# Reading k head by head in halves of TensorE's array, and loading the first down weights later, in linear attention with two feed-forward blocks

## The chip, the core and the metric

The kernel runs on one core of one Trainium2 chip. The metric is the device time of one execution in microseconds (us). A profile is one such execution, recorded instruction by instruction; its span runs from the first to the last instruction.

## What is computed

For 4 batches of 8 heads, 576 positions and 64 features a head, all in float32: linear attention with a norm per head, then a gated feed-forward block (d_ff 1536), then a softplus one (d_ff 2048).

```python
kv = np.einsum('bhsd,bhse->bhde', k, v)
out = np.einsum('bhsd,bhde->bhse', q, kv)
rms = np.sqrt(np.mean(out * out, axis=-1, keepdims=True) + 1e-06)
x = out / rms * g_norm                 # then (2304 tokens, 512 features)
x = (silu(x @ w_gate) * (x @ w_val)) @ w_out
y = softplus(x @ w2_in) @ w2_out
```

The weights arrive as 64-bit floats.

## The kernel before

**Attention.** The 576 positions of a batch are four chunks of 128 (position p*4+c is row p of chunk c) and a rest of 64. `load_kv` loads k and v in two halves of four heads. `kv_step(b, hp)` (lines 311 to 340) makes the head pair hp's part of `kv = k^T v`: four matmuls (line 318) with two heads of k as the stationary 128x128 operand and two heads of v as the moving one, and one (line 327) over the rest of 64 rows. That gives a 128x128 block of which only the two 64x64 blocks on the diagonal are wanted; after the last pair ScalarE copies one (line 338) and VectorE the other (line 339) into `kv`. Float32 matmuls appear as two matmul records each in the profile, so a step is 8 records of line 318 and 2 of line 327.

**The order of k.** A matmul's stationary operand needs the two heads of one chunk side by side. For batches 0 and 1 k is loaded as it lies in memory (tile `kr`, head, chunk, feature) and reordered into `k` by a ScalarE copy (line 185) and a VectorE copy three times as long (line 186), whose places in the order are set by the table `K0`. For batches 2 and 3 four loads of short runs (line 192) do the ordering.

**The chain of a chunk.** `q_step` transposes q (tile `pq`, copied by ScalarE to `qt`, line 353), `o_step` multiplies by kv (tile `pa`, line 366), ScalarE squares (line 377, `sq`), VectorE sums (lines 380 and 381, `ss`), GpSimd raises to a power (line 382, `rs`), VectorE scales (line 386, `x`), (for the rests of two batches together, `o_step` writes the one batch's 64 rows into output partitions 0 to 63 by eight matmul records, then the other's into 64 to 127 by eight more: shape 128*64, x16), and `x_step` transposes back (line 397, `px`) and splits into a high and a low part (`xh` line 403 on ScalarE, `xl` line 404 on VectorE). All products of the feed-forward blocks are three matmuls, high by high, low by high and high by low (`mm3`, line 436; `pg` gate, `pv` value, `py` down, `pz` the second block's down).

**Weights.** A weight tile (128x512, 512 KB) is loaded raw by `load_cols` or `load_rows` (tiles `gr`, `vr`, `or`), turned from 64-bit to float32 and split: ScalarE line 263, VectorE lines 266, 267 and 271 (`gz`, `vz`, `oz`), ScalarE line 282 (`gh`, `vh`, `oh`), GpSimd line 285 (`gl`, `vl`, `ol`). The raw tiles lie in the pool `stage`, of five buffers.

**What sets the order.** The program writes every engine's order out itself. Work off TensorE is put in a heap with a due time (`defer`), and TensorE's steps advance the clock of that heap by planned costs (`tick`). Batch 0's and half of batch 1's attention run first, by the tables; then `prepare` spreads the conversion of the down weights of chunk 0 and of the three tiles of chunk 1 over the time behind (`P0_AT`, `P0_EVERY`), and the feed-forward units of chunks 0 and 1 of a batch are woven with the attention of the next batches (`weave`). Loads are issued by SyncE (SP) in the order written; a load into a buffer waits for its last reader, and all loads behind it wait too.

Of the kernel before, what the change touches and what calls it, by code (L numbers as in the profile page):

```python
# [10 lines left out]
F32 = mybir.dt.float32  # L11
F32R = mybir.dt.float32r
I32 = mybir.dt.int32
I64 = mybir.dt.int64
# [4 lines left out]

K0 = [[4.0, 11.1], [16.08, 21.0]]
Q0 = [[9.4, 9.8, 10.2, 10.6], [25.0, 24.86, 25.4, 28.42]]
S0 = [6.5, 8.0, 12.9, 14.05, 10.7, 11.1, 11.5, 11.51, 14.9, 15.8, 15.78, 17.6, 23, 27.55, 25, 27.19]
S1 = [20.7, 21.9, 26.5, 27.76, 28]
# [12 lines left out]

P0_AT = 0.5
P0_EVERY = 2.09  # L40
P1_AT = 4.46
P1_EVERY = 9.21
SPLIT = 1.71
# [28 lines left out]
def tile_linear_attention_two_ffn(  # L72
# [19 lines left out]
    nc = tc.nc  # L92
    P = 128
    B, H, S, D = q.shape
# [34 lines left out]
    def defer(dt, f):  # L129
        heapq.heappush(queue, (now[0] + dt, next(serial), f))  # L130
# [29 lines left out]
    def load_kv(b, half):  # L160
        h0 = 4 * half
        if b == 1:

            if half == 0:
                kv_st["k", b] = accp.tile([P, 2, NC, 4, D], F32, tag="acc1", name="k1")
                kv_st["v", b] = xp.tile([P, 2, 4, NC * D], F32, tag="xh3", name="v1")
            kt, vt = kv_st["k", b][:, half], kv_st["v", b][:, half]
        else:
            pool, tag = (xp, f"x{'hl'[half]}2") if b == 0 else (stage, "stage")
            kt = pool.tile([P, NC, 4, D], F32, tag=tag, name=f"k{b}_{half}")  # L170
            vt = stage.tile([P, 4, NC * D], F32, tag="stage", name=f"v{b}_{half}")
        ks = k[b, h0:h0 + 4, 0:T, :]
        if b < 2:

            if b == 0:
                kr = xp.tile([P, 4, NC, D], F32, tag=f"x{'hl'[half]}4", name=f"kr{b}_{half}")
            else:
                if half == 0:
                    kv_st["raw"] = xp.tile([P, 2, 4, NC, D], F32, tag="xl3", name=f"kr{b}")
                kr = kv_st["raw"][:, half]  # L180
            nc.sync.dma_start(kr.rearrange("p h c d -> p h (c d)"), ks.rearrange("h (p c) d -> p h (c d)", p=P))
            ko = kr.rearrange("p h c d -> p c h d")

            def order():
                nc.scalar.copy(kt[:, 0:1], ko[:, 0:1])
                nc.vector.tensor_copy(kt[:, 1:NC], ko[:, 1:NC])

            defer(K0[b][half], order)
        else:
            ks = ks.rearrange("h (p c) d -> c p h d", p=P)  # L190
            for c in range(NC):
                nc.sync.dma_start(kt[:, c, :, :], ks[c])
        nc.sync.dma_start(vt, v[b, h0:h0 + 4, 0:T, :].rearrange("h (p c) d -> p h (c d)", p=P))
        kv_st["k", b, half] = kt
        kv_st["v", b, half] = vt

# [46 lines left out]
    def load_rows(w, nm, j):  # L243
        t = stage.tile([P, DM], I64, tag="stage", name=f"{nm}r{j}")
# [65 lines left out]

    def kv_step(b, hp):
        if hp == 0:
            kvps[b] = ps.tile([P, NP, P], F32, tag="ps", name=f"kvp{b}")
# [12 lines left out]
        j = 64 * (b % 2)  # L326
        nc.tensor.matmul(  # L327
            pk[:, hp, :],
            lhsT=r[0][j:j + 64, 2 * hp:2 * hp + 2, :].rearrange("p h d -> p (h d)"),
            rhs=r[1][j:j + 64, 2 * hp:2 * hp + 2, :].rearrange("p h d -> p (h d)"),  # L330
            start=False,
            stop=True,
        )
        tick(1.0)
        if hp == NP - 1:
            t = pages.tile([P, NP, P], F32, tag="pg", name=f"kv{b}")
            nc.gpsimd.memset(t, 0.0)
            nc.scalar.copy(t[0:64, :, 0:64], pk[0:64, :, 0:64])
            nc.vector.tensor_copy(t[64:128, :, 64:128], pk[64:128, :, 64:128])
            kvm[b] = t  # L340

    qts = {}
# [488 lines left out]
    with tc.manual_schedule():  # L831
# [65 lines left out]
        for t in range(NT - 1):  # L897
            if t + 1 < B:
                b = t + 2
                attn = side[t + 1][[len(S1), N2, N3][t]:]  # L900
                if b < B:
                    load_kv(b, 0)
                    load_kv_rem(b)
                    load_kv(b, 1)
                    load_q(b)
                    if b % 2:
                        load_q_rem(b // 2)
                    attn = attn + side[b][:[N2, N3][t]]
                weave(unit1(0, t) + unit1(1, t), (0, attn))
            else:  # L910
# [97 lines left out]
```

## Time and profile before

| | |
|---|---|
| median of 3 runs | 914.14 us (912.66 to 915.32) |
| profiled execution: device time | 911.74 us |
| profiled execution: span | 909.9 us |
| TensorE matmul (PE) busy | 885.3 us, 97% of the span |
| VectorE (DVE) busy | 589.3 us, 65% |
| ScalarE (ACT) busy | 353.0 us, 39% |
| GpSimd (POOL) busy | 288.2 us, 32% |
| chain that ended last, by engine | PE 85%, DVE 6% |

PE is the engine of the matmuls and PEld its loading of stationary operands. A row of the timeline gives start, duration, engine, line, operation, output tile and input tile; in brackets stands how long the engine was idle just before, and what ended that. The 24.6 us in which TensorE has no matmul lie for the larger part in the first 60 us.

### The profile page before, as it was taken

To read this page: it belongs to the slowest core of one execution; us is meant where nothing else is said; L and a number is where in the kernel's file an instruction comes from. 1 tells how busy PE (TensorE), PEld (TensorE's weight loads), DVE (VectorE), ACT (ScalarE), POOL (GpSimd) and SP (SyncE) were. 2 spreads that over 40 slices of the span, in tenths; PEclk is the share of its full clock that TensorE was granted. 3 is DMA by queue.
4 is the path that set the end of the run, shared out by engine and by line. 5 is a ranking of instruction groups with operands and counts; after the bars stand their busy time and mean duration, and the time that the engine had idled before them with its cause. 6 is when DMAs were issued, how large, how long until landed. Compare 5 with 4: busy or idle time off the path is not lost.

```text
span 909.9 us, 11710 instructions
## 1 busy us (share of the span) xinstructions
PE 885.3 (97%) x4352; PEld 741.3 (81%) x4352; DVE 589.3 (65%) x916; ACT 353.0 (39%) x615; POOL 288.2 (32%) x216
## 2 busy tenths in 40 slices
PE   6889999999999999999999999999998999999997
PEld 5668888888888888888888878888876888888886
DVE  2965357867778686778786745565688654545553
ACT  3634344332323323233333453444445443334340
POOL 0633211212122213131222453333544442444331
PEclk9999999999999999999999999999999999999999
DMA  9966202142342516060515043444433643333203
GB/s 271 254 138 125 93 1 70 47 162 88 121 151 81 169 63 208 1 231 24 185 69 210 24 138 139 139 155 165 167 126 129 232 138 139 106 127 107 103 1 115
DMA packets 83992, 114.00 MB, mean 125 GB/s; under 512 B 27616, under 2 KB 56288, under 8 KB 83680
## 3 DMA queue, kind: packets, MB, share of 16 engines
q1 hardware_dynamic: 83776, 113.27, 39.0%
q8 instruction: 34, 0.56, 0.3%
q14 instruction: 22, 0.18, 0.1%
q10 hardware_dynamic: 160, 0.00, 0.0%
HBM read 91.75 MB, written 21.50 MB: 124 GB/s over the span
## 4 chain that ended last, share of the span: by engine, by line
PE 85%; DVE 6%; issue 3%; POOL 2%; ACT 1%; DMA 1%; SPq 0%; POOLq 0%; DVEq 0%; ACTq 0%
PE pz L436 20%; PE pv L436 15%; PE pg L436 15%; PE py L436 15%; PE hY L436 8%; PE hZ L436 4%; PE hr L436 2%; PE hX L436 2%; PE pa L366 1%; PE kvp L318 1%; DMA kvr<-in_v_dram 1%; POOL b L620 1%; PE pq L349 1%; DVE yacc L496 1%; PE kvp L327 1%
## 5 line engine op out<-in xcount | busy, mean ns | idle before, releaser
L496 DVE TENSOR_TENSOR yacc<-yacc,py 128x512 f32<-128x512 f32 (+1 forms) x220 | 136.9, 630 | 53.7 <-PE py L436 53.1
L796 DVE TENSOR_TENSOR zacc<-zacc,pz 128x512 f32<-128x512 f32 x126 | 86.0, 684 | 109.4 <-PE pz L436 109.2
L698 POOL TENSOR_TENSOR gl<-c,gh 128x512 fp32r<-128x512 f32 x64 | 88.5, 1384 | 189.7 <-ACT gh L697 145.4
L436 PE MATMUL pz<-pl,gh 128*128 128x512 f32 x288 | 112.6, 391 | 2.0 <-POOL pl L285 2.0
L436 PE MATMUL pz<-ph,gl 128*128 128x512 f32 x288 | 112.5, 390 | 0.6 <-POOL gl L698 0.6
L436 PE MATMUL pz<-ph,gh 128*128 128x512 f32 x288 | 112.5, 391 | 0.0
L478 ACT CAST uh<-u 128x512 fp32r<-128x512 f32 (+1 forms) x60 | 34.7, 578 | 174.3 <-DVE u L475 174.3
L436 PE MATMUL hY<-b,wh 128*128 128x512 f32 x384 | 97.6, 390 | 0.9 <-DVE c L726 0.9
L436 PE MATMUL py<-uh,oh 128*128 128x512 f32 (+1 forms) x240 | 89.8, 374 | 1.3 <-DVE yacc L496 1.3
L436 PE MATMUL pv<-xh,vh 128*128 128x512 f32 (+1 forms) x240 | 90.1, 375 | 0.0
L436 PE MATMUL pg<-xh,gh 128*128 128x512 f32 (+1 forms) x240 | 90.0, 375 | 0.0
L436 PE MATMUL pg<-xl,gh 128*128 128x512 f32 (+1 forms) x240 | 88.6, 369 | 0.5 <-DVE xl L404 0.5
L436 PE MATMUL pv<-xh,vl 128*128 128x512 f32 (+1 forms) x240 | 88.7, 369 | 0.0
L436 PE MATMUL py<-uh,ol 128*128 128x512 f32 (+1 forms) x240 | 88.7, 369 | 0.0
L436 PE MATMUL pg<-xh,gl 128*128 128x512 f32 (+1 forms) x240 | 88.5, 369 | 0.0
L436 PE MATMUL py<-ul,oh 128*128 128x512 f32 (+1 forms) x240 | 88.4, 368 | 0.0
L436 PE MATMUL pv<-xl,vh 128*128 128x512 f32 (+1 forms) x240 | 88.4, 368 | 0.0
L436 PEld LDWEIGHTS hY<-b,wh 128*128 128x128 f32 x384 | 71.6, 188 | 15.8 <-DVE c L726 1.3
L436 PEld LDWEIGHTS pz<-pl,gh 128*128 128x128 f32 x288 | 54.2, 188 | 13.3 <-POOL pl L285 2.8
L436 PEld LDWEIGHTS pz<-ph,gl 128*128 128x128 f32 x288 | 54.1, 188 | 13.0 <-POOL gl L698 1.8
L479 DVE TENSOR_TENSOR ul<-u,uh 128x512 fp32r<-128x512 f32 (+1 forms) x60 | 38.9, 648 | 39.1 <-ACT uh L478 39.1
L436 PEld LDWEIGHTS pz<-ph,gh 128*128 128x128 f32 x288 | 54.2, 188 | 10.8 <-ACT ph L282 0.3
(115 smaller groups left out, 1644.3 us busy)
## 6 DMA issues: line engine op xcount, KB each, us to landing
pr<-in_moe_w_out_dram SPq DMA_DIRECT2D x32, 512.0 KB, 4.3
wh<-w2d SPq DMA_DIRECT2D x32, 512.0 KB, 4.2
wh<-w2d SPq DMA_DIRECT2D x64, 256.0 KB, 3.0
ir<-in_moe_w_in_dram SPq DMA_DIRECT2D x16, 512.0 KB, 5.9
w2d<-kh SPq DMA_DIRECT2D x32, 256.0 KB, 2.0
w2d<-kl SPq DMA_DIRECT2D x32, 256.0 KB, 2.5
gr<-in_moe_w_gate_dram SPq DMA_DIRECT2D x12, 512.0 KB, 5.7
vr<-in_moe_w_val_dram SPq DMA_DIRECT2D x12, 512.0 KB, 6.4
```

Source lines behind the costliest of these rows:

```text
L318: nc.tensor.matmul(pk[:, hp, :], lhsT=kt[:, c, i:i + 2, :].rearrange("p h d -> p (h d)"), rhs=vt[:, i:i + 2, c * D:(c + 1) * D], start=(c ...
L327: nc.tensor.matmul(pk[:, hp, :], lhsT=r[0][j:j + 64, 2 * hp:2 * hp + 2, :].rearrange("p h d -> p (h d)"), rhs=r[1][j:j + 64, 2 * hp:2 * hp ...
L349: nc.tensor.transpose(pq[:, hp, :], src[:, 2 * hp:2 * hp + 2, :].rearrange("p h d -> p (h d)"), ident)
L366: nc.tensor.matmul(pv[p0:p0 + n, hp, :], lhsT=qt[:, hp, p0:p0 + n], rhs=kvm[bb][:, hp, :], start=True, stop=True,)
L436: nc.tensor.matmul(dst, lhsT=a, rhs=b_, start=first and i == 0, stop=last and i == n - 1, skip_group_check=not check)
L478: nc.scalar.copy(uh, u)
L479: (nc.gpsimd if UL1 == "g" else nc.vector).tensor_sub(ul, u, f32(uh))
L496: defer(ADD1, lambda: nc.vector.tensor_add(a[:, d, :], a[:, d, :], p))
L620: (nc.gpsimd if BLO[n][int(i[1])] == "g" else nc.vector).tensor_sub(t[:, 1], src(), f32(t[:, 0]))
L698: nc.gpsimd.tensor_sub(lo, l, f32(hi))
L796: defer(ADD2, lambda: nc.vector.tensor_add(av[:, m, :], av[:, m, :], p))
```

## The change

Every batch's k is loaded as it lies in memory, in one load for a half, and the ordering copies of lines 185 and 186 and their table go. `kv_step` makes each head by itself: two matmuls of 64 stationary and 64 moving columns in the place of one of 128 and 128, the one head's into output partitions 0 to 63, the other's into 64 to 127. Of chunks 0 and 1 of the down weights the raw tiles are loaded behind the loads of the third batch, into the buffers of tile `xh2` and `xl2` and no longer into `stage`, and their conversion is due later (`O0_AT`, `O0_EVERY`); the gate and value weights of chunk 1 come earlier for it.

```diff
-K0 = [[4.0, 11.1], [16.08, 21.0]]
+O0_AT = 16.0
+O0_EVERY = 2.5
...
-            kt = pool.tile([P, NC, 4, D], F32, tag=tag, name=f"k{b}_{half}")
-            vt = stage.tile([P, 4, NC * D], F32, tag="stage", name=f"v{b}_{half}")
...
-            def order():
-                nc.scalar.copy(kt[:, 0:1], ko[:, 0:1])
-                nc.vector.tensor_copy(kt[:, 1:NC], ko[:, 1:NC])
...
-            for c in range(NC):
-                nc.sync.dma_start(kt[:, c, :, :], ks[c])
+            kt = pool.tile([P, 4, NC, D], F32, tag=tag, name=f"k{b}_{half}")
+            vt = stage.tile([P, 4, NC, D], F32, tag="stage", name=f"v{b}_{half}")
+        for t, src in ((kt, k), (vt, v)):
+            nc.sync.dma_start(
+                t.rearrange("p h c d -> p h (c d)"),
+                src[b, h0:h0 + 4, 0:T, :].rearrange("h (p c) d -> p h (c d)", p=P))
...
         for c in range(NC):
-            nc.tensor.matmul(
-                pk[:, hp, :],
-                lhsT=kt[:, c, i:i + 2, :].rearrange("p h d -> p (h d)"),
-                rhs=vt[:, i:i + 2, c * D:(c + 1) * D],
-                start=(c == 0),
-                stop=False,
-            )
+            for e in range(2):
+                nc.tensor.matmul(
+                    pk[D * e:D * e + D, hp, :],
+                    lhsT=kt[:, i + e, c, :],
+                    rhs=vt[:, i + e, c, :],
+                    start=(c == 0),
+                    stop=False,
+                )
...
-        load_rows(w_out, "o", 0)
         load_cols(w_gate, "g", 1)
         load_cols(w_val, "v", 1)
-        load_rows(w_out, "o", 1)
...
-        prepare(w1(0)[2:] + w1(1), None, P0_AT, P0_EVERY)
+        prepare(w1(1)[:2], None, P0_AT, P0_EVERY)
+        prepare([w1(0)[2], w1(1)[2]], None, O0_AT, O0_EVERY)
...
+                        load_rows(w_out, "o", 0, xp, "xh2")
+                        load_rows(w_out, "o", 1, xp, "xl2")
```

How that moves the instructions is seen at three places. On TensorE, at the first two head pairs of batch 2 among the value matmuls of chunk 1 (`pv`), before:

```order
L436 MATMUL pv_0_633<-xl_335,vh_476 128x512
L318 MATMUL kvp_640<-v_0_385,k_0_384 128x128 x4
L327 MATMUL kvp_640<-kvr_1_392,kvr_0_391 128x128
L436 MATMUL pv_0_633<-xh_334,vh_476 128x512
L436 MATMUL pv_0_633<-xh_334,vl_477 128x512
L436 MATMUL pv_0_633<-xl_335,vh_476 128x512
L318 MATMUL kvp_640<-v_0_385,k_0_384 128x128 x4
L327 MATMUL kvp_640<-kvr_1_392,kvr_0_391 128x128
```

and after:

```order
L421 MATMUL pv_0_642<-xl_350,vh_460 128x512
L302 MATMUL kvp_651<-v_0_410,k_0_409 64x64 x8
L312 MATMUL kvp_651<-kvr_1_414,kvr_0_413 64x64 x2
L421 MATMUL pv_0_642<-xh_349,vh_460 128x512
L421 MATMUL pv_0_642<-xh_349,vl_461 128x512
L421 MATMUL pv_0_642<-xl_350,vh_460 128x512
L302 MATMUL kvp_651<-v_0_410,k_0_409 64x64 x8
L312 MATMUL kvp_651<-kvr_1_414,kvr_0_413 64x64 x2
```

Nothing else moves on TensorE: each of the 16 steps has twice as many matmuls, of half the width, at the same place. On VectorE, at batch 1's chunks 1 to 3 (`x`, `ss`, `xl`), before:

```order
L266 TENSOR_SCALAR vz_478<-vz_478 128x512
L267 SCALAR_TENSOR_TENSOR vz_478<-vr_170,vz_478 128x512
L386 TENSOR_TENSOR x_1_509<-pa_1_443,rs_1_451 128x512
L271 SCALAR_TENSOR_TENSOR vz_478<-vr_170,vz_478 128x512
L404 SCALAR_TENSOR_TENSOR xl_522<-px_0_515,gcol,xh_521 128x4x128
L266 TENSOR_SCALAR oz_513<-oz_513 128x512
L267 SCALAR_TENSOR_TENSOR oz_513<-or_172,oz_513 128x512
L386 TENSOR_TENSOR x_2_540<-pa_2_469,rs_2_484 128x512
L380 TENSOR_REDUCE ss_3_534<-sq_3_533 128x8
L381 TENSOR_SCALAR ss_3_534<-ss_3_534 128x8
L271 SCALAR_TENSOR_TENSOR oz_513<-or_172,oz_513 128x512
L404 SCALAR_TENSOR_TENSOR xl_522<-px_1_554,gcol,xh_521 128x4x128
```

and after, from the same x of chunk 1 on:

```order
L371 TENSOR_TENSOR x_1_526<-pa_1_466,rs_1_474 128x512
L389 SCALAR_TENSOR_TENSOR xl_534<-px_0_528,gcol,xh_533 128x4x128
L371 TENSOR_TENSOR x_2_549<-pa_2_492,rs_2_503 128x512
L365 TENSOR_REDUCE ss_3_543<-sq_3_542 128x8
L366 TENSOR_SCALAR ss_3_543<-ss_3_543 128x8
L389 SCALAR_TENSOR_TENSOR xl_534<-px_1_561,gcol,xh_533 128x4x128
L371 TENSOR_TENSOR x_3_587<-pa_3_537,rs_3_544 128x512
L365 TENSOR_REDUCE ss_4_581<-sq_4_580 128x8
L366 TENSOR_SCALAR ss_4_581<-ss_4_581 128x8
L460 TENSOR_TENSOR u_0_592<-s_0_512,pv_0_521 128x512
L464 TENSOR_TENSOR ul_0_595<-u_0_592,uh_0_594 128x512
L389 SCALAR_TENSOR_TENSOR xl_534<-px_2_602,gcol,xh_533 128x4x128
```

No conversion stands between them any more; the six rows of `oz` now come together behind the last `xl` of batch 1, in front of chunk 1's `u` of batch 0. On SyncE's queue, from the loads of q's rest on, before:

```order
L230 DMA qr_163<-in_q_dram 64x8x64 x2
L245 DMA or_166<-in_moe_w_out_dram 128x512
L240 DMA gr_168<-in_moe_w_gate_dram 128x4x128
L240 DMA vr_170<-in_moe_w_val_dram 128x4x128
L245 DMA or_172<-in_moe_w_out_dram 128x512
L192 DMA k_0_384<-in_k_dram 128x4x64 x4
L193 DMA v_0_385<-in_v_dram 128x4x256
```

and after:

```order
L213 DMA qr_160<-in_q_dram 64x8x64 x2
L223 DMA gr_163<-in_moe_w_gate_dram 128x4x128
L223 DMA vr_165<-in_moe_w_val_dram 128x4x128
L174 DMA k_0_409<-in_k_dram 128x4x256
L174 DMA v_0_410<-in_v_dram 128x4x256
L187 DMA kvr_0_413<-in_k_dram 64x8x64
L187 DMA kvr_1_414<-in_v_dram 64x8x64
L174 DMA k_1_417<-in_k_dram 128x4x256
L174 DMA v_1_418<-in_v_dram 128x4x256
L205 DMA q_421<-in_q_dram 128x8x64 x4
L228 DMA or_426<-in_moe_w_out_dram 128x512
L228 DMA or_428<-in_moe_w_out_dram 128x512
```

The two down weights have moved behind all of batch 2, and a half of k is one load in place of four.

## Rows read from the trace of the kernel before

**Rows 1.** The page: busy us, share and count; busy tenths in 40 slices.

```profile
PE 885.3 (97%) x4352; PEld 741.3 (81%) x4352; DVE 589.3 (65%) x916; ACT 353.0 (39%) x615; POOL 288.2 (32%) x216
...
PE   6889999999999999999999999999998999999997
```

**Rows 2.** Two stages of 10 us: length, busy us of each engine, granted clock, DMA.

```profile
40.00:50.00 10.00, 8.83 (x64) 7.12 (x63) 8.67 (x16) 7.41 (x14) 6.87 (x5) 1.00 0.85 172
50.00:60.00 10.00, 6.70 (x38) 5.21 (x37) 7.57 (x13) 4.07 (x7) 6.56 (x5) 1.00 0.97 172
```

**Rows 3.** Timeline of TensorE, 34 to 59 us: three of its waits.

```profile
35.04 0.50 PE L436 MATMUL pg<-xl,gh 128*128 128x512 f32 x1 [0.50 <-DVE xl L404]
...
47.60 0.66 PE L397 MATMUL px<-ident,x 128*128 128x128 f32 x4 [0.44 <-DVE xl L404]
...
58.33 0.66 PE L397 MATMUL px<-ident,x 128*128 128x128 f32 x4 [3.30 <-DVE x L386]
```

**Rows 4.** Chain that ended last: matmuls of batch 0's kv (start, us, what).

```profile
9.89 2.00 PE kvp L318 x8
...
16.18 0.90 PE kvp L318 x8
...
18.58 0.43 PE kvp L327 x2
```

**Rows 5.** Timelines of VectorE and GpSimd, 11 to 31 us.

```profile
11.91 0.76 DVE L218 COPY q<-qr 128x512 f32<-128x512 f32 x2 [6.23 <-DMA qr<-in_q_dram]
...
28.81 0.94 DVE L186 COPY k<-kr 128x768 f32<-128x768 f32 x1
29.67 1.28 DVE L386 TENSOR_TENSOR x<-pa,rs 128x512 f32<-128x512 f32 x2
...
27.85 1.94 POOL L382 TENSOR_TENSOR rs<-ss,mhalf 128x8 f32<-128x8 f32 x1 [0.18 <-DVE ss L381]
```

**Rows 6.** Timelines of PE, ACT, DVE and POOL, 48 to 58 us: batch 1's rest.

```profile
48.88 1.58 PE L366 MATMUL pa<-kv,qt 128*64 128x128 f32 x16
...
51.05 0.62 ACT L282 CAST oh<-oz 128x512 fp32r<-128x512 f32 x1 [1.96 <-DVE oz L271]
...
53.16 0.68 DVE L380 TENSOR_REDUCE ss<-sq 128x8 f32<-128x512 f32 x1
...
55.19 1.64 POOL L382 TENSOR_TENSOR rs<-ss,mhalf 128x8 f32<-128x8 f32 x1 [0.17 <-DVE ss L381]
...
57.59 0.68 DVE L386 TENSOR_TENSOR x<-pa,rs 128x512 f32<-128x512 f32 x1
```

**Rows 7.** Tile oz, 34 to 56 us: durations in ns, least, median, most.

```profile
L266 DVE TENSOR_SCALAR oz<-oz x2: 422/630/837, 35.8 to 47.5; 128x512 int32<-128x512 int32 x2
L267 DVE SCALAR_TENSOR_TENSOR oz<-or,oz x2: 691/692/693, 36.3 to 48.3; 128x512 int32<-128x512 int32 x2
L271 DVE SCALAR_TENSOR_TENSOR oz<-or,oz x2: 684/686/687, 38.2 to 50.3; 128x512 int32<-128x512 int32 x2
```

**Rows 8.** Chain that ended last, where TensorE never waits.

```profile
90.59 0.70 PE pv L436 x3
91.29 0.89 PE kvp L318 x8
92.18 0.41 PE kvp L327 x2
92.60 0.89 PE py L436 x3
...
115.09 1.51 PE pa L366 x16
```

**Rows 9.** Tile pa in two short stretches: matmul and load records present.

```profile
115.07:115.51 0.44, 0.44 (x5) 0.44 (x5) 0.00 (x0) 0.00 (x0) 1.00 0.00 0
115.51:115.90 0.39, 0.39 (x10) 0.39 (x9) 0.00 (x0) 0.00 (x0) 1.00 0.00 0
```

**Rows 10.** Timeline of SyncE's queue: q of batch 2.

```profile
47.36 4.97 SPq L222 DMA_DIRECT2D q<-in_q_dram  x4
```

More of the change, by code (lines that the diff above doesn't have):

```diff
@@ L164, in load_kv @@
             if half == 0:
-                kv_st["k", b] = accp.tile([P, 2, NC, 4, D], F32, tag="acc1", name="k1")
-                kv_st["v", b] = xp.tile([P, 2, 4, NC * D], F32, tag="xh3", name="v1")
+                kv_st["k", b] = accp.tile([P, 2, 4, NC, D], F32, tag="acc1", name="k1")
+                kv_st["v", b] = xp.tile([P, 2, 4, NC, D], F32, tag="xh3", name="v1")
             kt, vt = kv_st["k", b][:, half], kv_st["v", b][:, half]
         else:
-            pool, tag = (xp, f"x{'hl'[half]}2") if b == 0 else (stage, "stage")
-            kt = pool.tile([P, NC, 4, D], F32, tag=tag, name=f"k{b}_{half}")
-            vt = stage.tile([P, 4, NC * D], F32, tag="stage", name=f"v{b}_{half}")
[L172 to L182, printed above, removed]
-            def order():
-                nc.scalar.copy(kt[:, 0:1], ko[:, 0:1])
-                nc.vector.tensor_copy(kt[:, 1:NC], ko[:, 1:NC])
-            defer(K0[b][half], order)
-        else:
-            ks = ks.rearrange("h (p c) d -> c p h d", p=P)
-            for c in range(NC):
-                nc.sync.dma_start(kt[:, c, :, :], ks[c])
-        nc.sync.dma_start(vt, v[b, h0:h0 + 4, 0:T, :].rearrange("h (p c) d -> p h (c d)", p=P))
+            pool, tag = (xp, f"x{'hl'[half]}4") if b == 0 else (stage, "stage")
+            kt = pool.tile([P, 4, NC, D], F32, tag=tag, name=f"k{b}_{half}")
[4 more added lines that the diff above has]
+                src[b, h0:h0 + 4, 0:T, :].rearrange("h (p c) d -> p h (c d)", p=P))
         kv_st["k", b, half] = kt
@@ L241, in load_cols, with load_rows @@
         raw[nm, j] = t.rearrange("p c f -> p (c f)").bitcast(I32).rearrange("p (n t) -> p n t", t=2)
-    def load_rows(w, nm, j):
-        t = stage.tile([P, DM], I64, tag="stage", name=f"{nm}r{j}")
+    def load_rows(w, nm, j, pool=None, tag="stage"):
+        t = (pool or stage).tile([P, DM], I64, tag=tag, name=f"{nm}r{j}")
         nc.sync.dma_start(t, w[j * P:(j + 1) * P, :])
@@ L312, in kv_step @@
         if hp == 0:
-            kvps[b] = ps.tile([P, NP, P], F32, tag="ps", name=f"kvp{b}")
+            kvps[b] = ps.tile([P, NP, D], F32, tag="ps", name=f"kvp{b}")
         pk = kvps[b]
@@ L317, in kv_step @@
         for c in range(NC):
-            nc.tensor.matmul(
-                pk[:, hp, :],
-                lhsT=kt[:, c, i:i + 2, :].rearrange("p h d -> p (h d)"),
-                rhs=vt[:, i:i + 2, c * D:(c + 1) * D],
-                start=(c == 0),
-                stop=False,
-            )
+            for e in range(2):
[6 more added lines that the diff above has]
+                )
         r = kvr[b // 2]
         j = 64 * (b % 2)
[L327 to L333, printed above, removed]
+        for e in range(2):
+            nc.tensor.matmul(
+                pk[D * e:D * e + D, hp, :],
+                lhsT=r[0][j:j + 64, 2 * hp + e, :],
+                rhs=r[1][j:j + 64, 2 * hp + e, :],
+                start=False,
+                stop=True,
+            )
         tick(1.0)
@@ L337, in kv_step @@
             nc.gpsimd.memset(t, 0.0)
-            nc.scalar.copy(t[0:64, :, 0:64], pk[0:64, :, 0:64])
-            nc.vector.tensor_copy(t[64:128, :, 64:128], pk[64:128, :, 64:128])
+            nc.scalar.copy(t[0:64, :, 0:64], pk[0:64])
+            nc.vector.tensor_copy(t[64:128, :, 64:128], pk[64:128])
             kvm[b] = t
@@ L907, in tile_linear_attention_two_ffn @@
                         load_q_rem(b // 2)
+                    else:
+                        load_rows(w_out, "o", 0, xp, "xh2")
+                        load_rows(w_out, "o", 1, xp, "xl2")
                     attn = attn + side[b][:[N2, N3][t]]
```

## Prediction

> **What bounds the kernel now.** I read first the page: TensorE's matmuls are busy 97% of the span, and its row of slices is full from the fourth slice (68 us) almost to the end [rows 1]. Behind that point only less TensorE time can shorten the kernel; ahead of it TensorE waits, and what it waits for counts. The windows of 10 us show how much: between 50 and 60 us it has matmuls for 6.70 us, 3.30 idle, and between 40 and 50 for 8.83 [rows 2]. The timeline of TensorE then names the waits: 0.50 us until the last `xl` of batch 0, 0.44 us until an `xl` of batch 1, and 3.30 us until an `x` [rows 3]. The last is the x of batch 1's rest, whose transpose stands behind chunk 1's gate matmuls; all of the idle time of that window is this one wait. The shorter waits between these are for ScalarE's copies of q; a gate or value conversion takes the down one's place ahead of those copies, so I leave them as they are.
>
> **The sum, part by part.**
>
> *A. Ordering copies.* The VectorE copies of batch 0 stand where VectorE has nothing else to do, and the transposes of q that follow are held by q itself: q's copies end at 11.91 + 0.76 = 12.67 us [rows 5]. The second half of batch 1's copies does count. It takes 28.81 to 29.67 on VectorE, and only then come the two x, the second at 30.27 us (half of the 1.28 us later) [rows 5]. It can't come as early as the copy is long, since it needs the fourth `rs`: that ends at 29.79 and itself waited 0.18 us for VectorE's `ss` [rows 5], which the other half's copy delays. So the x can come at 29.79 - 0.18 = 29.6 and not at 30.27: 0.6 us, which all of batch 0's `xl` and the 0.50 us wait [rows 3] pass on. Bounds: 0.5 (no gain on `ss`) to 0.9 (the whole copy).
>
> *B. The second half of batch 0's kv.* From 16.18 to 18.58 + 0.43 = 19.01 us TensorE works on two steps, 2.83 us [rows 4], and the copies of kv, the first products and GpSimd's chain of `rs` hang behind them. What a step costs afterwards is the disputed price of this change, so first that.
>
> *The price of a step in halves.* Before, 8 records take 0.89 us, 0.111 each; the two of the rest 0.41 where 2 x 0.111 = 0.22 would do; and the next three products 0.89 where they take 0.70 elsewhere [rows 8]. So a change of the array's shape costs 0.19 us, and there are two of them in a step: 0.89 + 0.41 + 0.19 = about 1.50 us. Afterwards there are three, as the four chunks (128 rows by 64 columns) and the rest (64 by 64) differ from the big products and from each other: 0.57 us, and 16 + 4 = 20 records of some length t each, so 0.57 + 20t. A record of 64 moving columns should take half of one of 128: 0.055 us. Whether the two halves of the array work at one time decides the rest. The one place where this trace uses halves is the product of the rests: 16 records, eight in the one half and then eight in the other, in 1.51 us [rows 8], where 16 x 0.111 + 0.19 = 1.97 would be one after the other. The short windows show where that comes from: in 0.44 us while only the first half works there are 5 matmuls and 5 loads, in the 0.39 us where the two meet 10 and 9 [rows 9]. Matmuls and loads of the two halves go on beside each other, at twice the rate. The new order alternates between the halves after every two records, better than eight and eight. So t has bounds of 0.028 (fully beside each other) and 0.055 (one after the other); I take 0.030, near the lower, because that is what the meeting half of those rows does. A step is then 0.57 + 0.60 = 1.17 us, 0.33 less than 1.50.
>
> The Trainium skill, in "TensorE: Matmul & The Clock Gate", section "Part 3: Packing small matmuls", says that loads overlap with matmuls in flight only when the row group differs, and here the two halves share all rows. By that rule a load and a matmul of 0.055 each would follow one another, t = 0.11, and a step would cost 2.8 us. The trace disagrees where it can be asked: in the second window loads and matmuls of two column halves fill the same 0.39 us [rows 9].
>
> *B, then.* Two steps next to each other have four changes of shape within and 40 records: 0.76 + 40t = 1.96 us at t = 0.030, 0.9 less than 2.83. At t = 0.055 it is 2.96, a loss of 0.1. The first two steps of batch 0 are hidden by q's arrival (above), batch 1's four by the chain of A; were that cover gone, each would be worth the same 0.33.
>
> *C. Conversions of the down weights.* Two tiles cost VectorE 2 x (0.63 + 0.69 + 0.69) = 4.0 us between 35 and 51 us [rows 7], in a stretch where it is busy 8.67 of 10 us [rows 2], and they stand in the chain to the long wait: the product of the rests ends at 48.88 + 1.58 = 50.46; ScalarE's cast of `oh` waits 1.96 us for `oz` and only starts at 51.05, and the square stands behind it; `ss` starts at 53.16, `rs` at 55.19 behind GpSimd's two low parts, the x at 57.59 [rows 6]. Without the conversions I rebuild the chain, with 0.62 us for each step on ScalarE, 0.68 for each on VectorE and 1.64 for `rs`, as the cast, the `ss`, the x and the `rs` of [rows 6] take: square, `ss`, then on VectorE chunk 0's u, its low part (a cast on ScalarE between) and an `xl`, beside which `rs` is done, then x. That is 2 x 0.62 + 5 x 0.68 = 4.6 us and, estimated, 0.5 for the small step behind `ss` and the hand-overs: 5.2 us from the product's end to the transpose, against 58.33 - 50.46 = 7.9 before; TensorE has 58.33 - 3.30 - 50.46 = 4.6 us of its own to do in that time. So 0.6 of the 3.30 us stays and 2.7 is gained; bounds 1.5 (`rs` still queued behind one low part of 1.3) and 3.3. The 0.44 us before it waits for an `xl` that stands directly behind a value conversion; with that done earlier I count it as gained: 0.4.
>
> The 4.0 us of conversions now stand behind the last `xl` of batch 1, in front of chunk 1's u. That u needs the value product, whose 12 matmuls (0.23 us each [rows 8]) lie behind the transpose with batch 2's four steps (1.2 each) among them: 7.5 us, so 3.5 us of cover. If that went, u and the down product behind it would be late by as much. Their loads are queued behind batch 2's q, four issues in 4.97 us [rows 10]. The v ahead of q now waits for the buffer of the gate weight, whose last step takes the place of the first `oz` one, 38.2 + 0.7 = 38.9 us [rows 7]; with 5 us for q the two are issued near 45 us. They are wanted near 54, where TensorE ends chunk 1's gate product; what a load takes to land isn't in these rows, but it has 9 us.
>
> *D. The eight steps of batches 2 and 3.* They lie where TensorE never waits: 8 x 0.33 = 2.6 us. At t = 0.055: 0.57 + 1.10 = 1.67, a loss of 8 x 0.17 = 1.4. The single loads of k cost nothing on this path, as those steps already found k there.
>
> Sum: 0.6 + 0.9 + 2.7 + 0.4 + 2.6 = 7.2 us. The profiled execution, 911.74 us with a span of 909.9, would take 904.5; it lies 2.4 below the median of the runs, 914.14, from which the sum gives **906.9 us**. I call 0.3%, 2.7 us, the least that a measurement tells from no change: below 911.4 is faster, above 916.9 slower.
>
> **The rivals.**
>
> *Halves one after the other* (t = 0.055). Everything of A and C comes (3.7), B loses 0.1 and D 1.4: 2.2 us gained, 911.9 us, no change by the bound. For it speaks that no row here shows records as short as 64 columns; against it rows 9.
>
> *A sequencer that can't hand out records so fast.* A step is 40 instructions with the loads; the closest that records stand in this trace is about 0.055 us in the meeting stretch [rows 9]. If handing out is the limit, t lies at 0.055 or somewhat above, and the time near the last rival's. The Trainium skill, same page, section "Back-to-back issue gap", gives 62 ns a matmul with hardware decode off; by that the gain would be 0.8 us and the time 913.3. No row here decides it.
>
> *Slower.* A record in halves can't hide its load and keeps today's 0.109 to 0.111 us. Then eight steps cost 0.57 + 20 x 0.109 = 2.75 each, 10.0 us more, and B 0.76 + 4.36 - 2.83 = 2.3 more; with A and C's 3.7 back that is 8.6 slower, 922.7 us. The general form is a loss of 200t - 9.5 against 3.7 gained: from t = 0.066 on the change is no gain, from 0.080 slower by the bound.
>
> *The long wait hardly shrinks*, because `rs` on GpSimd and not VectorE holds it: C 1.5 in place of 2.7, 908.1 us.
>
> *A cold start.* The granted clock is 1.00 in the rows that I read [rows 2, 9], yet eight records take 2.00 us at 9.89 and 0.90 at 16.18 [rows 4]: until then TensorE works at the lower of its two levels, 1.2 of 2.4 GHz. Shorter matmuls between 6 and 12 us leave more idle time before q arrives, and the rise could come later. If batch 0's products (32 records, 3.6 us at the full level) fell to the lower level by half, the chain to `rs` starts 1 to 2 us later: 908 to 909 us.
>
> **How the numbers follow.** Likeliest, as summed: 0.58, its own range 904.5 (t = 0.028, the long wait gone, a run at the quick end of those shown) to 908.5. Long wait hardly shrinks: 0.10; cold start: 0.06. Halves in series or handing out as the limit: 0.20, of which a fifth falls just below 911.4. Slower: 0.06. Faster is then 0.58 + 0.10 + 0.06 + 0.04 = 0.78, the same 0.16, slower 0.06. The range reaches from 904.0 to 912.0, up to the rival of halves in series.
>
> **What would show it.** Right: a step among the big products as one row of 16 records in well under 0.7 us and one of 4; the transpose of batch 1's rest waiting under 1 us; batch 0's first `pg` with `xl` near 33.5 us and not 35.04; TensorE's busy time lower by about 2 to 3 us behind 60 us. Wrong: 16 records in 0.9 us or more (series), gaps of "issue" within them (handing out), or that transpose still idle for 2 us with GpSimd named.

## The result, and the profile after

The changed kernel takes 905.33 us (median of 4 runs, 904.67 to 906.78) beside 913.4 us for the kernel before in the same session: ratio 0.9912, 95% interval 0.9889 to 0.9935, so faster by 8.1 us. Run again on another chip (the ninth kernel below) it took 906.53 us, ratio 0.9938 (0.9923 to 0.9953). The gain differs between the two sessions (8.1 and 4.9 us) mostly through the kernel before, whose runs differ with TensorE's mean granted clock: in the second session it took 911.06 to 911.46 us in six runs at a mean of 1.000 and 914.72 in one at 0.995, in the first none is below 912.14. The profiled execution after took 905.19 us with a span of 903.4, 6.5 less than before.

The page of the kernel after, TensorE's busy time and its slices, answers to [rows 1]; the windows under it to [rows 2] (length, busy us of PE, PEld, DVE, ACT and POOL, granted clock, DMA share, GB/s).

```profile
PE 877.4 (97%) x4512; PEld 732.4 (81%) x4512; DVE 585.0 (65%) x912; ACT 351.6 (39%) x611; POOL 288.0 (32%) x216
...
PE   5799999999999999999999999999998999999997
```

```profile
20.00:30.00 10.00, 7.65 (x102) 6.56 (x100) 9.04 (x18) 4.55 (x8) 8.23 (x6) 1.00 1.12 319
30.00:40.00 10.00, 7.18 (x53) 5.67 (x52) 6.87 (x13) 5.83 (x11) 2.44 (x3) 0.83 0.99 257
40.00:50.00 10.00, 9.27 (x68) 7.66 (x67) 7.21 (x13) 6.23 (x11) 8.40 (x6) 1.00 1.05 260
50.00:60.00 10.00, 9.65 (x86) 7.20 (x86) 8.02 (x14) 5.40 (x9) 1.88 (x3) 1.00 0.19 62
```

Between 50 and 60 us TensorE has work for 9.65 us where it had 6.70, and between 40 and 50 for 9.27 where it had 8.83: term C. But between 30 and 40 the granted clock is 0.83, a mean over its two levels, and TensorE has 2.8 us without a matmul where it had 1.2. The timeline of TensorE shows both (brackets: idle time just before, and what ended it); it answers to [rows 3].

```profile
18.96 3.84 PE L351 MATMUL pa<-kv,qt 128*128 128x128 f32 x32 [0.99 <-DVE kv L324]
...
31.54 0.66 PE L334 MATMUL pq<-ident,q 128*128 128x128 f32 x4 [0.54 <-ACT q L201]
33.80 0.80 PE L421 MATMUL pg<-xh,gh 128*128 128x512 f32 x1 [1.60 <-ACT xh L388]
...
34.82 0.64 PE L421 MATMUL pg<-xl,gh 128*128 128x512 f32 x1
35.26 1.87 PE L351 MATMUL pa<-kv,qt 128*128 128x128 f32 x8
...
47.39 0.60 PE L382 MATMUL px<-ident,x 128*128 128x128 f32 x4
...
48.62 1.58 PE L351 MATMUL pa<-kv,qt 128*64 128x128 f32 x16
...
55.11 0.66 PE L382 MATMUL px<-ident,x 128*128 128x128 f32 x4 [0.35 <-DVE x L371]
```

The wait of 3.30 us is 0.35, and the one of 0.44 is gone. The transpose of batch 1's rest starts at 55.11 and not 58.33: 3.22 us. But the first gate product `pg` starts at 33.80, where it started at 33.83 before, and with `xl` at 34.82 for 35.04, not near 33.5: of the 1.5 us of A and B 0.2 has arrived there. In front of it stands a new wait of 1.60 us, and the eight records of `pa` take 1.87 us where they take 1.13 elsewhere.

Behind 60 us the chain of work shows a step among the big products, which answers to [rows 8]:

```profile
86.49 0.61 PE kvp L302 x16
87.10 0.26 PE kvp L312 x4
87.36 0.89 PE py L421 x3
88.25 0.61 PE kvp L302 x16
```

That is 0.61 + 0.26 + 0.19 (the three products behind take 0.89 for 0.70) = 1.06 us for 1.50, so 0.44 less in each, 8 x 0.44 = 3.5 us: term D. With 3.22 that makes 6.7 of the 6.5 us by which the span is shorter.

Where A and B went is read from three timelines (ScalarE, VectorE, GpSimd), which answer to [rows 5] in the first three lines and to [rows 6] in the last three:

```profile
30.87 0.62 ACT L201 COPY q<-qr 128x512 f32<-128x512 f32 x1 [2.72 <-DMA qr<-in_q_dram]
...
28.43 0.69 DVE L371 TENSOR_TENSOR x<-pa,rs 128x512 f32<-128x512 f32 x1 [0.33 <-POOL rs L367]
...
30.87 0.74 DVE L201 COPY q<-qr 128x512 f32<-128x512 f32 x1 [1.08 <-DMA qr<-in_q_dram]
...
50.30 0.60 ACT L362 ACTIVATE sq<-pa 128x512 f32<-128x512 f32 x1 [1.48 <-PE pa L351]
...
50.93 0.69 DVE L365 TENSOR_REDUCE ss<-sq 128x8 f32<-128x512 f32 x1
...
54.37 0.68 DVE L371 TENSOR_TENSOR x<-pa,rs 128x512 f32<-128x512 f32 x1
```

The last x of batch 0 comes at 28.43 us, earlier than the 29.6 that A alone promised, so A and B were there at this point. B can be seen at its source too: batch 0's first products start at 18.96 us, and before at 19.97. Then ScalarE and VectorE stand still, ScalarE for 2.72 us, for batch 1's q, whose copies are ahead of the next `xh` and `xl` in their order. The loads are later than before. From issue to landing the tile qr takes (least, median, most) before, and then after:

```profile
DMA to landing us min/median/max: 8.0/10.1/10.7
```

```profile
DMA to landing us min/median/max: 8.6/12.4/12.5
```

The view of the DMA queues shows one more piece there: code of an engine, 16 KB in one packet. Before it falls in the window 28 to 30 us, after in 20 to 22 (queue: packets, MB, share of 16 engines):

```profile
q8 instruction: 1, 0.02, 4.3%
```

```profile
q8 instruction: 1, 0.02, 3.6%
```

3.6% of 16 engines over 2 us is 1.15 us on one of them, in a stretch where the DMA engines are busy throughout (share 1.12 between 20 and 30 us). What is queued behind it on that engine would end as much later; q comes 1.8 us later (12.5 for 10.7), so the piece by itself doesn't account for all of it. This was not in the prediction; runs 8, 10 and 11 below bear on it.

### The profile page after: what moved, and what is told of

Its sections match the earlier page's. It is cut to its first block, busy times and chain, and to the rows that moved or that the text cites. A ratio compares the mean times of both kernels' runs of the same rounds, so it can differ in the third digit from the quotient of the medians.

```text
span 903.4 us, 12017 instructions
## 1 busy us (share of the span) xinstructions
PE 877.4 (97%) x4512; PEld 732.4 (81%) x4512; DVE 585.0 (65%) x912; ACT 351.6 (39%) x611; POOL 288.0 (32%) x216
## 4 chain that ended last, share of the span: by engine, by line
PE 85%; DVE 4%; issue 3%; ACT 2%; POOL 2%; SPq 2%; DMA 1%; POOLq 0%; DVEq 0%; ACTq 0%
PE pz L421 20%; PE pv L421 15%; PE pg L421 15%; PE py L421 15%; PE hY L421 8%; PE hZ L421 4%; PE hr L421 2%; PE hX L421 2%; PE pa L351 2%; DMA qr<-in_q_dram 1%; SPq L174 1%; POOL b L605 1%; PE px L382 1%; POOL gl L683 1%; DVE yacc L481 1%
```

## The experiments

Times are medians, each beside the kernel before on the same chip. Batch and term names are the prediction's.

**1. Only the down weights late** (C alone: copies of k and the whole array stay). The edit to the kernel before:

```diff
-        load_rows(w_out, "o", 0)
...
-        load_rows(w_out, "o", 1)
...
-        prepare(w1(0)[2:] + w1(1), None, P0_AT, P0_EVERY)
+        prepare(w1(1)[:2], None, P0_AT, P0_EVERY)
+        prepare([w1(0)[2], w1(1)[2]], None, O0_AT, O0_EVERY)
...
+                        load_rows(w_out, "o", 0, xp, "xh2")
+                        load_rows(w_out, "o", 1, xp, "xl2")
```

> The kernel before with only the down weights of chunks 0 and 1 loaded and converted later; copies of k and the whole array are kept. If term C stands by itself (my theory), the transpose of batch 1's rest waits under 0.6 us in place of 3.30, the 0.44 us wait goes too, and the run is 3.0 to 3.4 us faster than before: ratio about 0.9965. If GpSimd's powers hold that transpose (first rival), or the gain came through the earlier start of the chain, under 1.5 us: ratio 0.9985 or more.

908.52 us, ratio 0.9949 (0.9935 to 0.9963). The transpose on its timeline of TensorE:

```profile
54.77 0.66 PE L399 MATMUL px<-ident,x 128*128 128x128 f32 x4 [0.35 <-DVE x L388]
```

58.33 - 54.77 = 3.6 us, the same as the spans give (909.9 and 906.3). C stands by itself, a little larger than expected.

**2. Only the halves** (the kernel before with its ordering copies; the heads of a pair as two matmuls):

```diff
-                pk[:, hp, :],
-                lhsT=kt[:, c, i:i + 2, :].rearrange("p h d -> p (h d)"),
-                rhs=vt[:, i:i + 2, c * D:(c + 1) * D],
...
+            for e in range(2):
+                nc.tensor.matmul(
+                    pk[D * e:D * e + D, hp, :],
+                    lhsT=kt[:, c, i + e, :],
+                    rhs=vt[:, i + e, c * D:(c + 1) * D],
```

> The kernel before with only the step in halves of the array, k still ordered by copies. My theory: 0.44 us less for each of the eight steps behind 60 us, 3.5 us, and up to 1.0 us more from batch 0's second half if nothing catches it: ratio 0.995 to 0.996, the long wait of about 3.3 us unchanged. Rival (the halves only pay because the copies went): the step is as short, but the run gains under 2 us, ratio above 0.998.

910.69 us, ratio 0.9978 (0.9965 to 0.9990), less than expected: 2.2 us between the medians. The profiled execution, one of the quicker of eleven (908.62 to 912.92), has a span of 906.3, 3.6 less: as much as D alone. The transpose of batch 1's rest comes where it came before, although batch 0's first products start 1.07 us earlier, at 18.90. Its window of 28 to 32 us (the columns of [rows 2]) and that transpose:

```profile
28.00:32.00 4.00, 3.96 (x31) 3.39 (x32) 3.67 (x5) 1.90 (x5) 3.81 (x4) 0.50 1.16 263
```

```profile
58.14 0.66 PE L399 MATMUL px<-ident,x 128*128 128x128 f32 x4 [3.29 <-DVE x L388]
```

The granted clock is 0.50, the lower of the two levels (1.2 of 2.4 GHz), in all four of these us; in the kernel before it is 1.00.

**3. Half by half** (the changed kernel; the eight records of the one head, then those of the other):

```diff
-        for c in range(NC):
-            for e in range(2):
+        for e in range(2):
+            for c in range(NC):
```

> The changed kernel with the eight records of one half first and then the eight of the other, in place of two and two. If the halves only work beside each other when the order alternates (my theory, with some overlap where they meet, as in the product of the rests), 16 records take 0.70 to 0.80 us in place of 0.61, and the run is 0.7 to 1.6 us slower than the changed kernel. If the order doesn't matter, 0.61 and no difference. If they were wholly in series, 0.93 and 2.6 us.

907.23 us, ratio 0.9939 (0.9919 to 0.9958). The chain of work:

```profile
88.03 0.90 PE kvp L302 x16
88.93 0.26 PE kvp L312 x4
89.19 0.90 PE py L421 x3
```

0.90 us and not 0.61, and longer than the 0.70 to 0.80 expected. The starts of the single records in the two traces, told apart by their spacing, show why. In either kernel a half takes a record every 0.058 us. Where the program alternates, the other half's record starts 0.007 us behind it, so there are two in 0.058 us, 0.029 each. Half by half, the second half's first record starts at 88.247 us and the first half's last at 88.417: only there, for the last three or four records of the one half and the first of the other, do both work. Two short windows show it as [rows 9] did (matmul records present, then loads):

```profile
88.10:88.20 0.10, 0.10 (x4) 0.10 (x4) 0.00 (x0) 0.00 (x0) 1.00 0.00 0
88.40:88.50 0.10, 0.10 (x9) 0.10 (x6) 0.00 (x0) 0.00 (x0) 1.00 0.00 0
```

So with the same instructions the order decides how far the halves work beside each other: throughout where they alternate, and at the seam alone where they don't. The prediction's rival of halves in series comes for the larger part by the order alone.

**4. q's copies behind** (the changed kernel; batch 1's q copies behind all `xh` and `xl` of batch 0):

```diff
-Q0 = [[9.4, 9.8, 10.2, 10.6], [25.0, 24.86, 25.4, 28.42]]
+Q0 = [[9.4, 9.8, 10.2, 10.6], [27.8, 28.4, 28.41, 28.42]]
```

> The changed kernel with the copies of batch 1's q standing behind all of batch 0's xh and xl. If the new wait for the load of q (1.60 us ahead of the first gate product) and the fall of the clock behind it ate the gains A and B (my theory), that product starts near 32.2 and not 33.80, the granted clock stays at 1.00 from 30 to 40 us, and the run is 2.5 to 3.5 us faster than the changed kernel, near 902.3. If the next wait takes over (rival), or the clock falls anyway, under 1 us.

906.23 us, ratio 0.9923 (0.9908 to 0.9938): no gain over the changed kernel. The wait for `xh` is gone, but another stands in its place:

```profile
34.66 0.66 PE L334 MATMUL pq<-ident,q 128*128 128x128 f32 x4 [1.04 <-ACT q L201]
```

In this execution batch 0's first products started at 20.10 us and not 18.96, and the granted clock is 0.60 in the window 28 to 32 us. So the gain expected of it did not come: the wait went on to the next product.

**5. Waits filled** (the changed kernel; 20 matmuls, 40 records, whose result nothing reads):

```diff
+    def fill(n):
+        t = po.tile([P, P], F32, tag="po", name=f"fill{next(fills)}")
+        for i in range(n):
+            nc.tensor.matmul(t, lhsT=ident, rhs=ident, start=True, stop=True)
```

> The changed kernel with 20 matmuls of the identity by itself (40 records, about 0.11 us each) put in front of four places at which TensorE waits in the profile after: 4 before the first product of batch 0 (wait 0.99 us), 5 before batch 1's first step (1.19), 4 before the second x transpose (1.16), 7 before the first gate matmul (1.60). Their result is read by nothing. If the fall of the granted clock near 33 us, by idle time that the shorter steps leave, is what takes A and B back: the clock stays at 1.00 throughout, the pa behind the first gate matmuls takes 1.13 us in place of 1.87, and the kernel is 1 to 2 us faster than the changed one, 903.5 to 904.5 us. Rival, the pace between 33 and 40 us is set by q's copies and not by the clock: the clock stays at 1.00 and the time at 905 to 906. Rival, the fills stand in the way: 906 to 907.

904.49 us, ratio 0.9914 (0.9902 to 0.9926). Four of its five runs have a mean clock of 0.999 or 1.000 and take 904.26 to 904.50; no run of the changed kernel, ten in all, is above 0.998. The timeline of TensorE:

```profile
33.87 0.50 PE L433 MATMUL pg<-xh,gh 128*128 128x512 f32 x1
...
35.28 1.13 PE L361 MATMUL pa<-kv,qt 128*128 128x128 f32 x8
...
54.40 0.66 PE L394 MATMUL px<-ident,x 128*128 128x128 f32 x4 [0.35 <-DVE x L381]
```

The clock is held and `pa` takes 1.13 us again. Yet `pg` starts at 33.87: its start is not a matter of the clock but of q, copied from 30.93 us on here too. Batch 1's rest is transposed at 54.40 us and not 55.11. Beside the 905.33 and 906.53 of the changed kernel the time is 1 to 2 us less, but the two were not run on one chip.

**6. Waits filled and q's copies behind** (5 and 4 together).

> The fills of the last run and batch 1's q copies behind all xh and xl. If clock and q's late load each hide the other, both removed bring A's and B's 1.5 us: 902.5 to 903.5 us, faster than either alone. If the stage is bound by its loads (348 GB/s until 30 us), q's arrival near 31 us holds the next product wherever the copies stand: no better than the fills alone, within 1 us.

905.21 us, ratio 0.9918 (0.9904 to 0.9932); the three of six runs at 0.999 or more take 903.61 to 904.12. So with the clock held the later copies are worth some 0.4 us; over all runs nothing can be told. q still holds the transpose, and the third line shows that the fills themselves are now in the way:

```profile
29.14 1.26 ACT L400 ACTIVATE xh<-px,gcol 128x512 fp32r<-128x512 f32 x2 [0.78 <-PE px L394]
...
31.73 0.66 PE L342 MATMUL pq<-ident,q 128*128 128x128 f32 x4 [1.32 <-ACT q L201]
32.23 1.73 PE L295 MATMUL fill<-ident 128*128 128x128 f32 x14
33.71 0.47 PE L433 MATMUL pg<-xh,gh 128*128 128x512 f32 x1
```

The last `xh` is there at 30.40 us, but the 14 records that were to fill the wait for it stand between the transpose and the first gate product and keep TensorE until 33.71. So this run doesn't show what the later copies are worth without them; it may be up to 1.5 us more.

**7. Down weights at the old place** (the changed kernel without C: the edit of 1 undone).

> The changed kernel with the down weights loaded and converted at the old place: k as loaded and halves alone. By the prediction's terms A, B and D as measured (0.6 + 0.9 + 3.5 = 5.0): 907.9 us by the kernel before at 912.9. If A and B are given back between 24 and 39 us: D alone, 909.0 to 910.5 us, the same as with halves and the copies kept (910.7) within 1 us, and the transpose of batch 1's rest waits about 3.3 us again.

910.47 us, ratio 0.9973 (0.9962 to 0.9985): not the 907.9 that A, B and D would give, but what the halves alone gave. Three windows of its profile and its transpose:

```profile
28.00:32.00 4.00, 4.00 (x32) 3.11 (x30) 2.28 (x4) 1.32 (x4) 3.37 (x4) 0.50 1.15 265
56.00:60.00 4.00, 2.04 (x7) 1.85 (x8) 2.73 (x5) 2.26 (x4) 0.93 (x2) 0.61 0.07 19
60.00:64.00 4.00, 4.00 (x27) 2.68 (x26) 0.58 (x1) 0.00 (x0) 0.00 (x0) 0.54 0.00 0
```

```profile
57.96 1.12 PE L382 MATMUL px<-ident,x 128*128 128x128 f32 x4 [3.32 <-DVE x L371]
```

The clock falls a second time here, behind the wait of 3.32 us, so the time of this run isn't set by the early stage alone. The transpose itself comes 0.37 us earlier than the 58.33 of the kernel before: that much of the 1.5 us has arrived there.

**8. Waits filled in the kernel before** (the edit of 5).

> The kernel before with the same 20 matmuls of the identity at the same four places. Its profile shows the clock at 1.00 there, so if the fills help only by the clock: no gain, 912.5 to 913.5 us, or up to 1 us slower where they stand in the way. If they help here as much as in the changed kernel, it isn't the halves' idle time that they fill.

913.50 us, ratio 1.0011 (1.0003 to 1.0020): the fills don't help where the clock does not need them, and they cost something: at a mean clock of 1.000 the two runs take 912.42 and 912.81 us, the kernel before on this chip 910.63 to 911.27. They show something else. 20 more matmuls bring the piece of code forward to the window 24 to 26 us, and with k ordered by copies and the whole array q now lands 12.5 us after its issue, as in the changed kernel, and ScalarE waits for it:

```profile
31.20 0.62 ACT L218 COPY q<-qr 128x512 f32<-128x512 f32 x1 [1.12 <-DMA qr<-in_q_dram]
```

**9. The changed kernel again**, for the three behind it.

> The changed kernel once more, unaltered, so that the other kernels of this call are compared with it on one chip: 904.7 to 906.0 us. Each theory expects the load of TensorE's code in the window 20 to 22 us and batch 1's q landing near 30.8 us again.

906.53 us (904.40 to 908.38), above the 904.7 to 906.0 expected. The piece of code falls in 20 to 22 us again, and q is copied from 31.25 us on. Its mean clock is 0.993 to 0.998; two windows of its profile, and its timeline of TensorE at batch 0's last steps and at the transpose of batch 1's rest:

```profile
28.00:32.00 4.00, 3.60 (x30) 3.04 (x31) 3.04 (x5) 1.74 (x4) 4.00 (x4) 0.57 1.18 264
688.00:692.00 4.00, 4.00 (x13) 3.16 (x13) 1.76 (x3) 1.15 (x2) 0.00 (x0) 0.68 0.00 0
```

```profile
16.20 1.12 PE L302 MATMUL kvp<-v,k 128*64 128x64 f32 x16
...
19.80 3.84 PE L351 MATMUL pa<-kv,qt 128*128 128x128 f32 x32 [0.99 <-DVE kv L324]
...
54.73 0.66 PE L382 MATMUL px<-ident,x 128*128 128x128 f32 x4 [0.35 <-DVE x L371]
```

The row of 16 records takes 1.12 us at the lower level and 0.69 at the upper, so TensorE rose later here than in the first profile, and batch 0's products start 0.84 us later (19.80 and 18.96): 0.17 us earlier than in the kernel before, which is what is left of B at its source.

**10. Halves in batches 2 and 3 alone** (C and D; `kv_step` and the loads of batches 0 and 1 as in the kernel before, with copies and the whole array):

```diff
     def kv_step(b, hp):
+        if b < 2:
...
+                kvps[b] = ps.tile([P, NP, P], F32, tag="ps", name=f"kvp{b}")
...
+        else:
...
+                kvps[b] = ps.tile([P, NP, D], F32, tag="ps", name=f"kvp{b}")
```

> Batches 0 and 1 as in the kernel before (ordered by copies, whole array), batches 2 and 3 as in the changed one, down weights late: terms C and D without A and B. If A and B bring nothing because a load of TensorE's code, which its greater number of instructions calls for earlier, holds up v and q: the code load stays in the window 28 to 30 us, q lands 10.5 to 10.7 us after its issue, and the time is the changed kernel's within 0.7 us, 904.5 to 906.0. If A and B bring the 1.5 us that the prediction gave them: 906.5 to 907.0 us.

905.50 us (905.16 to 906.48), ratio 0.9930 (0.9918 to 0.9942), on the chip of run 9 with its 0.9938. Without A and B it is no slower than with them; A and B as forecast would have made run 9 faster than this by 1.5 us. The code falls in 26 to 28 us, earlier than expected, and q lands 11.3 us after its issue, between the 10.7 and 12.5 of the others. TensorE:

```profile
33.23 0.50 PE L470 MATMUL pg<-xh,gh 128*128 128x512 f32 x1
...
34.43 0.49 PE L470 MATMUL pg<-xl,gh 128*128 128x512 f32 x1 [0.46 <-DVE xl L438]
...
54.10 0.66 PE L431 MATMUL px<-ident,x 128*128 128x128 f32 x4 [0.34 <-DVE x L420]
```

The gate starts even earlier than in the changed kernel, with the longer steps ahead of it. Part of that is the execution's luck: batch 0's products start at 19.36 us here, and with the same work ahead of them at 19.97 in the kernel before and 20.02 in run 1.

**11. Code brought forward by tiny matmuls** (the kernel before; 22 matmuls of two columns, read by nothing, ahead of the first step):

```diff
+        tiny = po.tile([P, 2], F32, tag="po", name="tiny")
+        for i in range(22):
+            nc.tensor.matmul(tiny, lhsT=ident, rhs=ident[:, :2], start=True, stop=True)
```

> The kernel before with 22 matmuls of two moving columns (44 records) at the very start, where TensorE waits for k; their result is read by nothing. They take no time from anything, but bring the load of code forward. If the load of code holds up the loads behind it: it falls between 18 and 23 us and not in 28 to 30, batch 1's q lands 12 us or more after its issue, as in all kernels with halves, and its copies on ScalarE start near 30.9 and not 29.7; the time rises by 0.5 to 1.5 us. If q's late landing comes from the halves themselves or from k read as loaded: 10.7 us as before, and no change in time.

917.01 us, ratio 1.0051 (1.0035 to 1.0067). The time can't be used, since the tiny matmuls did take time: 0.217 us a record, for two columns, and they hold up the first step to 10.76 us, where it starts at 6.76 in run 10:

```profile
1.36 9.55 PE L853 MATMUL tiny<-ident 128*128 128x2 f32 x44 [1.36 <-POOL ident masks.py:199]
10.76 2.05 PE L318 MATMUL kvp<-v,k 128*128 128x128 f32 x8
```

What it shows of the loads stands: with the code in the window 22 to 24 us the tile qr takes 12.5 us (median) to land, 12.7 at most, with whole array and copies.

**12. q ahead** (the changed kernel; batch 1's q loaded ahead of its second half of k and v, the last two steps behind the x transposes, q's copies as in 4):

```diff
-S1 = [20.7, 21.9, 26.5, 27.76, 28]
+S1 = [20.7, 21.9, 27.6, 27.7, 28]
...
+        load_q(1)
         load_kv(1, 1)
-        load_q(1)
```

> The changed kernel with batch 1's q loaded ahead of its second half of k and v, the last two kv steps behind the x transposes, and q's copies behind all xh. If q's landing alone holds the first gate matmul at 33.8 us: q lands near 29, the gate starts near 32.9, and the kernel is 0.7 to 1.2 us faster than the changed one, about 904.3 us. If the stage is held by the sum of its loads, the second half of v lands near 31 instead and its steps wait: no change or up to 1 us slower.

906.76 us, ratio 0.9938 (0.9924 to 0.9953): no gain. The row of q's transpose says why:

```profile
34.57 0.66 PE L334 MATMUL pq<-ident,q 128*128 128x128 f32 x4 [1.04 <-ACT q L201]
```

q was there (11.0 us after an issue at 16.54), but its ScalarE copy now stood behind that of kv, which waited for the delayed steps. So this run moved the wait and doesn't test the landing by itself.

## Why the prediction was right, and where not

906.9 us was forecast, 7.2 us gained; measured were 8.1 and, in the second session, some 5. The spans of the two profiled executions differ by 6.5. The size is near, but in part by luck: D brought 0.9 us more than its term, and A and B, 1.5 us of the sum, brought nothing that counts.

**C** (2.7 + 0.4 us forecast) came with 3.22 in the profile after, where batch 1's products ahead of it are 0.40 us late (the last full chunk's `pa` at 45.29 us for 44.89), and 3.6 alone (run 1). The rebuilt chain of the last x was right to 0.3 us: 5.2 us forecast from the product's end to the transpose, 55.11 - (48.62 + 1.58) = 4.9 seen, with `rs` hidden beside u, its low part and `xl`. The 0.44 us went as well. The rival that GpSimd holds `rs` is out. The conversions moved behind the last `xl` cost nothing that counts.

**D** (2.6 us) came with 3.5. The mechanism is the one of [rows 9], alternating halves beside each other; the term was mis-sized: a step takes 1.06 us, not 1.17. The records are as forecast, 0.029 us each by their starts in the trace (t = 0.030); it is the three changes of shape that were put too high: (1.06 - 20 x 0.029) / 3 = 0.16 us each and not 0.19. Run 3 rules out that 64-column records overlap as well in any order. The Trainium skill's rule in "TensorE: Matmul & The Clock Gate", "Part 3: Packing small matmuls", that loads overlap matmuls in flight only when the row group differs, does not hold here: both halves share all rows, 16 loads and 16 matmuls take 0.61 us, and the trace starts each load 0.003 us after the matmul before it in the same half. The 62 ns that the Trainium skill, in the same page's "Back-to-back issue gap", gives for a matmul with hardware decode off would make 16 matmuls alone 16 x 0.062 = 0.99 us, an estimate by its figure; the 0.61 us of the row show that this case is not the one here.

**A and B** (0.6 + 0.9 us) are where it failed. A's step "0.6 us, which all of batch 0's `xl` and the 0.50 us wait pass on" took the chain as free behind the x, and it was not: the x came early, and then met q. Runs 9 and 10, on one chip, show that the two terms bring nothing in sum (906.53 us with them, 905.50 without). What took them is read from the traces and only in part tested:

- *The clock*, for a part. Every profile with halves in batches 0 and 1 and no fills has a stretch between 24 and 40 us with the granted clock well below 1.00 (0.50 to 0.68 in one window of 4 us, in runs 2, 3, 4, 7, 9, 12 and the first); the kernel before and runs 1, 5, 6, 8, 10 and 11 stay at 1.00 there. Run 5 held it with work that does nothing else. Its runs at 0.999 to 1.000 take 904.26 to 904.50 us where run 10's at 0.999 take 905.16 and 905.24, so by these 0.8 of the 1.5 us are there then; the kernel before takes 910.63 to 911.27 us at 1.000 on the one chip and 911.06 to 911.46 on the other. By the profiles it is less: the transpose of batch 1's rest comes at 54.77 us with C alone (run 1), at 55.11 with A and B, and at 54.40 with A, B and the clock held, 0.4 earlier than with C alone. Run 10 has it at 54.10, from its early start; between executions of the same work half a microsecond is luck, so a closer division can't be had from these rows. The rival of a cold start named the cause, shorter matmuls that leave TensorE idle, but looked for it at the rise alone. The later rise occurs as well, in runs 4, 9 and 12 (products at 19.8 to 20.1 us).
- *q's landing*, for the rest; this is argued, not isolated. The shorter steps need twice the instructions, and TensorE's next 16 KB of code are loaded at 20 to 22 us and not 28 to 30. Runs 8 and 11, without any halves, show q late when the code is early; run 10 shows the code later again where batches 0 and 1 keep the whole array. Over the profiles with q's load at its old place: with the piece between 20 and 25 us (ten of them) q takes 11.9 to 12.7 us, at 27.9 (run 10) 11.3, at 28.6 and 28.7 (the kernel before and run 1) 10.7 and 10.5. That the piece is TensorE's code is inferred: in all fourteen profiles it starts when TensorE has begun 100 to 127 matmul records, whenever that is, and its queue brings 34 pieces for the 4352 matmuls of the kernel before and 35 for the 4512 of the changed one. The Trainium skill, in "Runtime: NRT & Kernel Launch", section "Instruction fetch mechanics", says that code comes in blocks of 16 KiB over the engine's own DMA queue and calls the cost mostly hidden; the block's size agrees with the trace (0.02 MB), and no wait of TensorE for it shows there, but the loads land later.

How the 1.5 us divide between the two is not settled: no run had the halves, a full clock and q on time together, and in run 6, which was meant to come near it, the fills took the place of the wait. Halves in series (0.20) and slower (0.06) did not come: a step takes 1.06 us and not 1.67 or more.

## What to carry to other kernels

A shorter step ahead of a stage that waits for loads was worth nothing here: look at what the freed chain meets next, here copies in an engine's fixed order behind a load that had just been on time. Two column halves of the array run beside each other if matmuls alternate between them, and for the most part one after the other if they don't, at the same count of instructions. Count instructions too: twice as many of them brought the next load of code forward, into the stage where every DMA engine is taken. And before two runs are compared to half a microsecond, look for a fall of the granted clock that has nothing to do with the change.

## What the runs showed of the hardware

- 16 records of 64 stationary and 64 moving columns take 0.61 us alternating between the halves and 0.90 us half by half. In either order a half takes a record every 0.058 us; alternating, the other half's stands beside it (0.029 each).
- A change of the array's shape costs 0.16 us here, worked out from a step of 1.06 us with three of them and 20 records.
- A piece of 16 KB of code occupies one DMA engine for 1.15 us (3.6% of 16 in 2 us), and a load in flight then lands 11.9 to 12.7 us after its issue in place of 10.5 to 10.7.
- A float32 matmul of two moving columns costs 0.217 us a record early in run 11, where one of 128 columns costs 0.25 (2.00 us for 8 in [rows 4]).
- The spread between runs of one kernel goes with the mean granted clock: the kernel before took 911.06 to 911.46 us at a mean of 1.000, 914.72 at 0.995. A second fall, near 688 us (0.68 over 4 us in run 9), occurs in some executions, in runs 3, 4, 9, 10 and 12, behind a stretch with 2.3 to 2.5 us of matmuls in 4; the first profile has the same stretch (2.30 us) and no fall. It costs 1.6 us: from the last `pv<-xh,vh` of the gated block to the end it is 388.5 us in runs 9 and 10 (from 516.2 and 515.5 us on), 386.9 in the first profile and run 5 (from 516.5 and 515.8 on).
